# A smaller first piece, and kv spread by SBUF DMAs, in a fused polysketch attention and feed-forward kernel

## The chip, the cores and the metric

The kernel runs on one core of a Trainium2 chip. The metric is device time in microseconds (us) of one execution, as the median of several runs. PE is the matrix engine (PEld its weight loads), DVE the vector engine, ACT the scalar engine, POOL the general engine, SP the engine that issues most DMAs.

## The reference

Attention with a quadratic feature map instead of a softmax, for 4 batches, 4 heads, 1088 tokens and head size 32, followed by a feed-forward block on the joined heads (4352 tokens, 128 columns, inner width 2048). S1 and S2 have 8 rows each.

```python
def phi(x):
    a = np.einsum('rd,bhsd->bhsr', S1, x)
    b = np.einsum('rd,bhsd->bhsr', S2, x)
    return np.einsum('bhsi,bhsj->bhsij', a, b).reshape(*x.shape[:-1], r * r)
q_p, k_p = (phi(q), phi(k))
kv = np.einsum('bhsf,bhsd->bhfd', k_p, v)
z = np.sum(k_p, axis=2)
num = np.einsum('bhsf,bhfd->bhsd', q_p, kv)
den = np.einsum('bhsf,bhf->bhs', q_p, z)[..., None] + 1e-06
x = (num / den)            # heads joined: (4352, 128)
h = x @ w_in
out = (h - np.tanh(h)) @ w_out
```

## The kernel before

The kernel records every operation with its reads and writes, and a table of tokens (TABLE) gives the order: "66t:0" puts operation 66 on the tensor engine and takes choice 0 of the buffer that it opens; v, a, g and s are DVE, ACT, POOL and SP; F and f are filler products of 512 and 256 columns. `plan` hands out the buffers in that order and `sync` sets the waits. Nothing is scheduled at run time: each engine works through its list in order, and SP's list is one queue of DMA issues. CAP limits the bytes of the large loads in flight: a load waits for the one that lies that many bytes back.

*Key side of a batch.* k is transposed in 32x32 blocks on DVE (kT, L536), PE makes the sketches a and b (L581), DVE transposes them back (abk, L593), PE makes the gram matrix for the denominator (L608, L618 or L620), DVE and POOL make the outer products w in three parts (L648), and PE multiplies them with v into a small matrix pv (L663), in which partitions are (head, v column) and columns the 64 features, in two halves of 32.

*kv_tail.* To use pv as the stationary matrix of the numerator, it has to be transposed, and each head's block is wanted on all four quadrants of 32 partitions, since the features of token block g lie on quadrant g. So ACT or DVE copies pv to kvd with each half repeated four times along the columns (128x256), PE transposes the two 128x128 halves (L681), and ACT or DVE copies the result to kvb.

*Query side.* q is transposed (L573), sketched by PE (L759), transposed back into abc (L764), divided by the denominator (L776 to L784), its outer products formed on POOL or DVE (qp, L802), transposed (qpT, L807), and the numerator formed by PE in 32x32 tiles: 32 products per batch, for two halves x of the features, four heads h (column strips of the array) and four token groups g (row strips), in the order x, h, g (L818). Two copies then write x transposed as bf16 into xT.

*Batch 0* is split: its first 12 column blocks (384 tokens) go through `q_heads`, which uses a block-diagonal kv made from pv by a DVE transpose (kvh, L691) and a masked product (kve, L692), and full-array products (L706, L737). The rest (192 columns per token group) takes the path of the other batches. So the feed-forward block can begin on 384 tokens.

*Feed-forward.* Groups of 384, 352, 352, six times 512, and 192 tokens (GCOLS). For each group and each of 16 blocks of the inner width: h (PE, L923) into one of three PSUM banks, tanh (ACT, L927), and, in an order of the table, the product with w_out (L944); the linear part h @ w_out comes from W_in x W_out made once (wc, L901, from transposed weights wiT, L887), as a high and a low bf16 part (L948). In groups 5 to 8 DVE adds h to tanh for some columns instead (L932). The output is transposed by DVE (ot, L953) and stored by four DMAs per group and batch.

*Fillers.* Before the feed-forward work begins PE runs products of zeros into bank 3 (L429, L430), 26 of 512 columns and 8 of 256; their operand zz is cleared by DVE first.

Of the kernel before, what the change touches and what calls it, by code (L numbers as in the profile page):

```python
# [4 lines left out]
B, H, S, D = 4, 4, 1088, 32  # L5
# [7 lines left out]
FP32 = mybir.dt.float32  # L13
# [5 lines left out]
GCOLS = [384, 352, 352] + [512] * 6 + [192]  # L19
CAP = 1.45e6  # L20
PAIRS = 7
GDIR = {5: 192, 6: 320, 7: 320, 8: 320}
CUT0 = [0, 12, 34]
PIECES = {0: [(3, 9)], 1: [(0, 9)], 2: [(0, 9)], 3: [(0, 9)]}
ENGINES = {"v": "vector", "a": "scalar", "g": "gpsimd", "t": "tensor", "s": "sync"}
TABLE = """
0v 15a 16s 18s 17s 56g 1g 10g 2g 14g 9g 13g 3g 6v 4v 5v 50v:0 12g 65g 58g 51v 54v 53v 52v 55g 7g 59g 19s 23s 22a 30s
21s F F F F F F F F F F F F 66t:0 84v 67t 69v:0 68t 70v F F F F f 71t:0 29s 20s 57g 8g 25s 72a:0 F f 73t 74a 24a 61g
27s 34s 64v 77v:0 76v:1 26s F F 85t:1 35s 78g:2 28s 107v 31s 75v 86v:0 87g:0 230a 88v:0 89v:0 90v:0 f 79t:0 80t 111t:0
81t 82v 33s F F F F F 238t:0 91v:0 92v:0 83g 229a 112v:1 42s 43s 32s 108a:0 95g:1 113g:0 96v:1 232g 40s 38s F f 237t  # L30
36s 39s 41s 114v:0 115v:0 f 109t f 93t:1 44s 37s 116g:0 239a 117g:0 119g:1 234g 231a f 97t:2 94v 110a:0 236g f 240t:0
124v:0 98a 45s 105s 100s 125v F 249t:1 250a:0 241t 253t:2 254a:1 251t:1 252a:2 233a 126t:0 255t:2 242v 48s 46s 257t:1
273t:0 128v:0 256a:3 281t:0 282t 283t 127v 279t:2 63g 129t:0 274a:4 259t:0 120v:0 258a:0 284t 261t:1 130v:0 118v 285t
280a:1 131t 243t:2 244t 99s 103s 101s 47s 102s 49s 104s 260a:2 262a:3 277t:0 263t:1 132v:0 121t:0 60g 133v 159v:0
278a:0 269t:0 160v 286t 136g:0 106s 264a:5 271t:1 235a 134v:1 123v 245t 122a 246t 270a:6 247a 161t:0 248v 135v:2
267t:0 265t:2 162v:1 272a:2 324t:1 266a:7 325a:8 62g 268a:9 137t:2 138t 139t 163v 169g:3 308t:1 170g:0 143v 140a:0
359t:0 309a:10 287t 288t 141t 360a:3 142a:0 316t:1 318t:2 317a:5 289t 275t:0 144t:0 178v 145v:0 146g:0 11g 147v:0
276a:7 319a:11 320t:1 290t 306t:0 291t 381t:2 292t 293t 321a:12 314t:1 307a:9 389t:0 382a:6 315a:2 294t 295t 304t:2
296t 390a:4 312t:1 305a:0 297t 298t 313a:7 299v:0 148v:0 332t:0 149v:0 164t:0 333a:1 165a:0 310t:2 311a:13 371t:1
336t:0 166t 367t:0 337t 328t:2 338t 339t 372a:0 167v:0 168v 322t:1 368a:14 329a:9 323a:10 179t:0 377t:0 330t:1 378a:13  # L40
150v:0 151v:0 326t:2 154g:1 327a:15 331a:16 340t 341t 342t 343t 152g:0 373t:0 374a:2 344t 387t:2 345t 180v:1 388a:5
334t:1 346t 335a:7 181g:0 347t 365t:0 348t 385t:2 366a:8 349t 386a:9 363t:1 350t 351t 352t 353t 369t:0 361t:2 155v
364a:1 153v 375t:1 376a:10 370a:7 362a:11 156t:0 383t:0 354v:1 379t:1 158a 391t:0 392t 182v:0 393t 157v 183v:0 394t
384a:12 430t:2 194v:0 380a:3 395t 418t:0 396t 431a:1 195v 414t:1 397t 444t:2 398t 399t 419a:8 400t 401t 436t:0 415a:0
402t 438t:1 403t 404t 184g:0 187v:0 213v 445a:2 432t:2 405t 406t 407t 408t 302s 437a:7 473t:0 439a:3 185g:1 433a:6
409v:2 428t:1 416t:2 171v:1 196t:0 474a:4 422t:0 446t:0 417a:5 429a:9 420t:2 434t:1 411s 172t:2 412s 197v:0 173t 198v
199t:0 174t 186v:0 189g:2 190v 205g:2 421a:10 424t:2 423a:0 435a:11 175a:0 200v:0 425a:12 447t 471t:0 472a:5 201t
440t:1 188v 176t 448t 426t:2 441a:13 357s 413s 410s 300s 489t:0 449t 450t 202v:0 203v 427a:8 490a:10 177v:0 442t:1
481t:2 214t:0 475t:0 451t 482a:0 443a:14 477t:2 206v:0 476a:15 452t 453t 487t:0 204v:1 478a:12 454t 499t:1 497t:2 455t
488a:8 456t 483t:0 457t 458t 215v:0 216v:0 217v:0 500a:9 218v:0 498a:16 469t:1 495t:2 459t 356s 219g:0 484a:1 485t:0  # L50
224v:0 225v:1 486a:6 470a:7 496a:11 191t:0 491t:0 222g:1 192v 220g:0 460t 493t:1 461t 462t 193a 524t:2 492a:17 463t
530t:0 223v 494a:3 479t:1 525a:13 464v:2 207t:0 465s 301s 531a:2 526v 208t 545t:2 501t:0 532v 536t:0 480a:14 527t:1
546a:18 221v 547v 537a:7 502t 503t 504t 538v 533t:2 505t 528a:5 506t 539t:0 529v 534a:4 507t 542t:1 540a:12 535v 508t
541v 543a:0 548t:2 509t 303s 510t 544v 560t:0 549a:1 511t 512t 554t:1 561a:14 550v 513t 562v 555a:6 551t:2 514t 552a:8
# [12 lines left out]
775t 791t:1 790t 776t 788t:0 792a:4 787t 803t:2 789a:0 802t 777t 778t 794t:1 793t 804a:5 808t:1 809t 799t:0 810t 800t
795a:1 801a:3 805t:2 806t 779v:1 780s 782s 807a:6 783s 811t 812t 813t 814t 815t 816t 781a 817t 818t 819t 820t 821t
822t 823t 824t 825t 826v:0 827s 829a 828s 830a
# [64 lines left out]
class _Prog:  # L134
# [40 lines left out]
    def plan(self, table, filler):  # L175
# [8 lines left out]
        for token in table.split():  # L184
            at += 1
            if token in "fF":
                o = _Op()
                o.engs, o.fn, o.mode, o.name, o.dma = {"tensor": 0}, filler[0][token], "128x128", "fill", 0
                o.deps, o.users, o.vals, o.lock, o.big = {filler[1]: True}, [], [], False, False
# [140 lines left out]
def bass_polysketch_attn__then__act_tanh_shrink_kernel(  # L330
# [27 lines left out]
    def copy(e, name, o, i):  # L358
# [32 lines left out]
    kvd_p = pool("kvd", 2, [128, 256])  # L391
# [4 lines left out]
    kvb_p = pool("kvb", 4, [128, 2, 128])  # L396
# [29 lines left out]
    zz = sbv("zz", [128, 384], BF16)  # L426

    zop = P.add({"vector": (1.0, 1.0)}, lambda e, n: e.memset(zz.ap[:, :], 0.0), w=[zz], name="zz")  # L428
    filler = ({"f": lambda e, n: e.matmul(bank(3)[:, 0:256], zz.ap[:, 0:128], zz.ap[:, 128:384], start=True, stop=True),  # L429
               "F": lambda e, n: e.matmul(bank(3), zz.ap[:, 0:128], zz.ap[:, None, 128:384].to_broadcast([128, 2, 256]),  # L430
                                          start=True, stop=True)}, zop)
    pb[3].ops.append(zop)
# [96 lines left out]
    kvbv = [_Val(kvb_p) for _ in range(B)]  # L529
# [142 lines left out]
    def kv_tail(b):  # L672
        kvd, kvb = _Val(kvd_p), kvbv[b]
        P.add({**_a(256), **_vp(256)}, lambda e, n: copy(
            e, n, kvd.ap.rearrange("p (x g f) -> p x g f", x=2, g=4),
            pv[b].ap[:, 0:64].rearrange("p (x f) -> p x f", x=2)[:, :, None, :].to_broadcast([128, 2, 4, 32])),
            r=[pv[b]], w=[kvd], name=f"kvd{b}")

        def kvt(e, n):
            for x in range(2):  # L680
                i = e.transpose(pv[b].ap[:, x * 128:(x + 1) * 128], kvd.ap[:, x * 128:(x + 1) * 128], ident.ap[:, :])  # L681
            return i
        P.add(_pe(260, 185.0), kvt, r=[kvd, ident], w=[pv[b]], mode="128x128", name=f"kvt{b}")
        P.add({**_a(256), **_vp(256)}, lambda e, n: copy(
            e, n, kvb.ap.rearrange("p x c -> p (x c)"), pv[b].ap[:, 0:256]),
            r=[pv[b]], w=[kvb], name=f"kvb{b}")

    kvh = _Val(ap=sb("kvh", [128, 64]))

    def kv_heads():  # L690
        P.add(_vp(64), lambda e, n: e.transpose(kvh.ap, pv[0].ap[:, 0:64]), r=[pv[0]], w=[kvh], name="kvh")  # L691
# [154 lines left out]
    def attention():  # L846
# [15 lines left out]
        for b0, b1 in PIECES[0]:  # L862
            q_piece(0, 3, b0, b1, *st)
# [178 lines left out]
```

## Time and profile before

| | |
|---|---|
| median of 3 runs | 104.08 us (103.92 to 104.67) |
| the profiled execution | 103.72 us, span 101.8 us |
| PE busy | 97.0 us (95% of the span) |
| DVE busy | 82.3 us (81%) |
| ACT busy | 80.1 us (79%) |
| POOL busy | 29.8 us (29%) |
| DMA | 11.37 MB, mean 112 GB/s |
| granted PE clock | 1.0 |

The span runs from the first to the last instruction. Lines such as L923 are lines of the kernel; a group of instructions is named by its line, its engine and operation, and the tiles out<-in. A product's length holds the time through the array, so lengths of neighbours overlap; the distance between starts is what a product costs in a stream. The chain of waits is followed back from the last instruction, at each step to what released it.

### The profile page before, as it was taken

How to read it: one execution, taken by the hardware profiler on the slowest of the kernel's cores; microseconds unless marked ns; L12 is line 12 of the kernel's file. 1: busy time of each engine (PE TensorE's matmuls, PEld its weight loads, DVE VectorE, ACT ScalarE, POOL GpSimd, SP SyncE). 2: the span in 40 equal slices, each digit the busy share in tenths (PEclk: the TensorE clock that was granted, in tenths of full speed). 3: DMA queues.
4: the chain of work that ended last, by engine and by line, in shares of the span. 5: the costliest groups of instructions: out<-in, count | busy, mean ns of one | idle time of the engine just before them, and what ended most of it. 6: DMA issues, size and time to landing. Idle time of an engine off the chain costs nothing.

```text
span 101.8 us, 3049 instructions
## 1 busy us (share of the span) xinstructions
PE 97.0 (95%) x1266; PEld 48.9 (48%) x1266; DVE 82.3 (81%) x148; ACT 80.1 (79%) x158; POOL 29.8 (29%) x50
## 2 busy tenths in 40 slices
PE   5999999999999999999999999999999999999960
PEld 2334666365744565554634454344453444444650
DVE  3449799699986996989998898688889788999530
ACT  0311257979799896998999799999979999989940
POOL 5130758963383292255501570000000000000000
PEclk9999999999999999999999999999999999999999
DMA  2898859999989300003400003106002640035445
GB/s 56 249 270 274 311 189 294 328 294 296 333 251 325 99 0 6 0 0 53 79 6 0 0 0 60 29 0 95 0 2 36 101 70 0 0 55 79 76 70 81
DMA packets 25917, 11.37 MB, mean 112 GB/s; under 512 B 19120, under 2 KB 23600, under 8 KB 25904
## 3 DMA queue, kind: packets, MB, share of 16 engines
q1 hardware_dynamic: 24528, 10.64, 40.6%
q10 hardware_dynamic: 1376, 0.54, 2.1%
q8 instruction: 10, 0.16, 0.7%
q14 instruction: 3, 0.02, 0.1%
HBM read 8.95 MB, written 2.23 MB: 110 GB/s over the span
## 4 chain that ended last, share of the span: by engine, by line
PE 95%; DVE 1%; ACT 0%; issue 0%
PE psb L923 31%; PE psb L944 29%; PE psb L430 9%; PE psb L818 6%; PE psb L663 5%; PE psb L581 3%; PE psb L948 3%; PE psb L759 3%; PE psb L737 1%; PE psb L608 1%; PE psb L901 1%; PE psb L429 1%; PE psb L681 1%; PE psb L706 1%; PE psb L887 1%; PE psb L618 1%
## 5 line engine op out<-in xcount | busy, mean ns | idle before, releaser
L927 ACT ACTIVATE th<-psb 128x512 bf16<-128x512 f32 (+3 forms) x135 | 70.3, 605 | 5.0 <-PE psb L923 4.3
L923 PE MATMUL psb<-xT,wi 128*128 128x512 bf16 (+3 forms) x160 | 47.3, 349 | 0.2 <-ACT th L927 0.2
L944 PE MATMUL psb<-th,wo 128*128 128x512 bf16 (+3 forms) x159 | 43.4, 347 | 0.0
L932 DVE TENSOR_TENSOR th<-psb,th 128x320 bf16<-128x320 f32 (+2 forms) x47 | 25.8, 558 | 4.5 <-ACT th L927 2.4
L923 PEld LDWEIGHTS psb<-xT,wi 128*128 128x128 bf16 x160 | 14.7, 98 | 22.8 <-ACT th L927 7.8
L944 PEld LDWEIGHTS psb<-th,wo 128*128 128x128 bf16 x159 | 15.3, 98 | 10.2 <-DVE ot L953 0.4
L802 POOL TENSOR_TENSOR qp<-ap,abc 128x768 f32<-128x768 f32 x8 | 12.0, 1511 | 6.9 <-DVE qp L802 5.4
L807 DVE STREAM_TRANSPOSE qpT<-qp 128x768 f32<-128x768 f32 x11 | 10.5, 962 | 0.2
L430 PE MATMUL psb<-zz 128*128 128x512 bf16 x26 | 9.3, 497 | 1.1 <-DVE zz L428 1.1
L648 POOL TENSOR_TENSOR w<-abk 128x768 f32<-128x768 f32 x5 | 7.5, 1517 | 8.4 <-DVE w L648 4.3
L953 DVE STREAM_TRANSPOSE ot<-psb 128x512 f32<-128x512 f32 (+3 forms) x10 | 6.2, 625 | 2.6 <-PE psb L944 2.6
L536 DVE STREAM_TRANSPOSE kT<-kL 128x576 f32<-128x576 f32 (+3 forms) x10 | 5.6, 600 | 1.4 <-DMA kL<-in_k_dram 1.4
L648 DVE TENSOR_TENSOR w<-abk 128x768 f32<-128x768 f32 x7 | 6.5, 947 | 0.1
L818 PE MATMUL psb<-qpT,kvb 32*32 32x288 f32 (+1 forms) x256 | 6.1, 392 | 0.0
L573 DVE STREAM_TRANSPOSE qT<-qL 128x1088 f32<-128x1088 f32 (+2 forms) x5 | 5.2, 1065 | 0.5 <-DMA qL<-in_q_dram 0.5
L663 PE MATMUL psb<-w,vL 128*32 128x64 f32 x288 | 5.4, 221 | 0.0
L764 DVE STREAM_TRANSPOSE abc<-psb 128x1152 f32<-128x1152 f32 (+1 forms) x4 | 5.0, 1262 | 0.4 <-PE psb L759 0.4
L663 PEld LDWEIGHTS psb<-w,vL 128*32 128x32 f32 x288 | 4.4, 110 | 2.0 <-issue 1.7
L430 PEld LDWEIGHTS psb<-zz 128*128 128x128 bf16 x26 | 2.8, 120 | 4.9 <-issue 3.1
L593 DVE STREAM_TRANSPOSE abk<-psb 128x288 f32<-128x288 f32 x8 | 3.4, 462 | 1.5 <-PE psb L581 1.5
L359 ACT ACT_TABLE_LOAD x1 | 1.3, 1283 | 4.2 <-DMA kL<-in_k_dram 4.2
L784 POOL TENSOR_TENSOR ap<-abc,rd 128x288 f32<-128x288 f32 (+1 forms) x3 | 1.9, 630 | 9.2 <-DVE rd L782 9.2
(90 smaller groups left out, 79.0 us busy)
## 6 DMA issues: line engine op xcount, KB each, us to landing
kL<-in_k_dram SPq DMA_DIRECT2D x8, 272.0 KB, 4.4
vL<-in_v_dram SPq DMA_DIRECT2D x15, 144.0 KB, 4.1
qL<-in_q_dram SPq DMA_DIRECT2D x6, 272.0 KB, 4.4
wo_f<-in_moe_w_out_dram SPq DMA_DIRECT2D x4, 256.0 KB, 4.1
out_dram<-ot SPq DMA_DIRECT2D x15, 64.0 KB, 2.0
wi_f<-in_moe_w_in_dram SPq DMA_DIRECT2D x3, 256.0 KB, 4.0
out_dram<-ot SPq DMA_DIRECT2D x8, 48.0 KB, 2.5
qL<-in_q_dram SPq DMA_DIRECT2D x2, 176.0 KB, 3.9
```

The source lines that it names most:

```text
L430: "F": lambda e, n: e.matmul(bank(3), zz.ap[:, 0:128], zz.ap[:, None, 128:384].to_broadcast([128, 2, 256]), start=True, stop=True)}, zop)
L536: P.add(_v(nb * 32 * (r1 - r0)), lambda e, n, e_=e_, nb=nb, r0=r0, r1=r1: e.transpose(kTv[b][r0].ap.rearrange("p (j u t r) -> p r j u t", ...
L648: P.add({**_v(768), **_gt(768)}, lambda e, n: e.tensor_tensor(out=wv.ap.rearrange("p (x i j) -> p x i j", i=8, j=8), in0=abh(0)[:, :, :, N ...
L663: i = e.matmul(pv[b].ap[h * 32:(h + 1) * 32, 0:64], vL[b][:, h, blk * 32:(blk + 1) * 32], wvs[b, p].ap[:, (bi * 4 + h) * 64:(bi * 4 + h + ...
L802: P.add({**_v(cn * 256), **_gt(cn * 256)}, lambda e, n, qp=qp, c0=c0, cn=cn: e.tensor_tensor(out=qp.ap[:, 0:cn * 256].rearrange("p (x i j) ...
L807: P.add(_v(cn * 256), lambda e, n, qp=qp, o0=o0, cn=cn: e.transpose(qt.ap[:, o0 * 256:(o0 + cn) * 256], qp.ap[:, 0:cn * 256]), r=[qp], w=[ ...
L818: i = e.matmul(psa4[h * 32:(h + 1) * 32, g, 0:nb * 32], kvb.ap[g * 32:(g + 1) * 32, x, h * 32:(h + 1) * 32], qq[g * 32:(g + 1) * 32, 0:nb, ...
L923: P.add(_mm(n_), lambda e, n, jb=jb, hv=hv: e.matmul(hv.ap[:, jb % m * 512:jb % m * 512 + n_], wi[jb // 4].ap[:, (jb % 4) * 128:(jb % 4 + ...
L927: act = P.add(_a(n_ * m), lambda e, n, hv=hv, th=th: e.activation(out=th.ap.rearrange("p (u x) -> p u x", u=m)[:, :, 0:n_], in_=hv.ap.rear ...
L932: P.add(_vp(gc * m), lambda e, n, hv=hv, th=th: e.tensor_tensor(out=th.ap.rearrange("p (u x) -> p u x", u=m)[:, :, 0:gc], in0=hv.ap.rearra ...
L944: fn = lambda e, n, x=x, st=st, sp_=sp_: e.matmul(ov.ap[:, 0:n_], wo[x // 4].ap[:, x % 4, :], ths[x][0].ap[:, ths[x][1] * 512:ths[x][1] * ...
L953: P.add(_vp(n_), lambda e, n: e.transpose(ot.ap[:, 0:n_], ov.ap[:, 0:n_]), r=[ov], w=[ot], name=f"ot{gi}")
```

## The change

1. `GCOLS` is 256, 416, 416 for the first three groups instead of 384, 352, 352. Batch 0's first piece is 8 column blocks (256 tokens) instead of 12, the rest 7 blocks (224 columns per token group) instead of 6.
2. `kv_tail` no longer repeats, transposes on PE and copies. DVE transposes pv in 32x32 blocks into slot 0 of a [128, 4, 64] tile (for batch 0 this is the kvh that existed already). Then six SBUF-to-SBUF DMAs per batch (128 - 32r and 32r partitions, 256 bytes per partition, for r = 1, 2, 3) fill slots 1 to 3 with the same rows shifted by r quadrants. The numerator takes head h for group g from slot (g - h) mod 4.
3. The numerator's 16 tiles are walked in another order in batches 0 (along diagonals), 2 (g outside, h inside) and 3 (reversed in the second half); batch 1 keeps h outside, g inside.
4. The fillers read a constant zero of one column, repeated, instead of zz, and wait for nothing. zz shrinks to 32 columns. 11 instead of 12 fillers stand ahead of the first k sketch.
5. CAP is 2.0 MB instead of 1.45 MB.
6. TABLE is new. The mask product wqd goes from DVE to POOL; one of batch 0's three w goes to DVE between the denominator and its reciprocal; the spread DMAs are on SP's queue, for batch 0 between the loads of k for batch 1 and those of w_out and k for batch 2; all four loads of w_in are on ACT's queue; the loads of the rest of q stand ahead of those of v. Both copies of wiT are on ACT, the casts of w_out are split over POOL, DVE and ACT, and all w of batches 1 to 3 are on POOL.

```diff
-GCOLS = [384, 352, 352] + [512] * 6 + [192]
-CAP = 1.45e6
+GCOLS = [256, 416, 416] + [512] * 6 + [192]
+CAP = 2.0e6
...
-CUT0 = [0, 12, 34]
-PIECES = {0: [(3, 9)], 1: [(0, 9)], 2: [(0, 9)], 3: [(0, 9)]}
+CUT0 = [0, 8, 34]
+PIECES = {0: [(2, 9)], 1: [(0, 9)], 2: [(0, 9)], 3: [(0, 9)]}
...
-    zz = sbv("zz", [128, 384], BF16)
+    zz = sbv("zz", [128, 32], BF16)
...
+    zc = nc.const_aps.tensor(0.0, [128, 1], FP32).bitcast(BF16)[:, 0:1]
+    fill = lambda n_: lambda e, n: e.matmul(bank(3)[:, 0:n_], zc.to_broadcast([128, 128]), zc.to_broadcast([128, n_]), start=True, stop=True)
+    filler = {"f": fill(256), "F": fill(512)}
...
-    kvbv = [_Val(kvb_p) for _ in range(B)]
+    kvbv = [_Val(ap=sb("kvb", [128, H, 64])) for _ in range(B)]
+    kvhv = [_Val(ap=x.ap[:, 0, :]) for x in kvbv]
...
     def kv_tail(b):
-        kvd, kvb = _Val(kvd_p), kvbv[b]
-        P.add({**_a(256), **_vp(256)}, lambda e, n: copy(
-            e, n, kvd.ap.rearrange("p (x g f) -> p x g f", x=2, g=4),
-            pv[b].ap[:, 0:64].rearrange("p (x f) -> p x f", x=2)[:, :, None, :].to_broadcast([128, 2, 4, 32])),
-            r=[pv[b]], w=[kvd], name=f"kvd{b}")
...
-        P.add(_pe(260, 185.0), kvt, r=[kvd, ident], w=[pv[b]], mode="128x128", name=f"kvt{b}")
-        P.add({**_a(256), **_vp(256)}, lambda e, n: copy(
-            e, n, kvb.ap.rearrange("p x c -> p (x c)"), pv[b].ap[:, 0:256]),
-            r=[pv[b]], w=[kvb], name=f"kvb{b}")
+        kvh, kvb = kvhv[b], kvbv[b]
+        if b:
+            P.add(_vp(64), lambda e, n: e.transpose(kvb.ap[:, 0, :], pv[b].ap[:, 0:64]), r=[pv[b]], w=[kvh], name=f"kvh{b}")
+        for r in range(1, H):
+            for j, (d0, s0, n_) in enumerate(((r * 32, 0, 128 - r * 32), (0, 128 - r * 32, r * 32))):
+                P.add({"sync": 480.0, "scalar": 400.0}, lambda e, n, r=r, d0=d0, s0=s0, n_=n_: e.dma_start(
+                    out=kvb.ap[d0:d0 + n_, r, :], in_=kvb.ap[s0:s0 + n_, 0, :]), r=[kvh], w=[kvb], dma=(n_ * 256, n_), name=f"kvs{b}.{r}{j}")
...
             for x in range(2):
-                for h in range(4):
-                    for g in range(4):
-                        i = e.matmul(psa4[h * 32:(h + 1) * 32, g, 0:nb * 32],
-                                     kvb.ap[g * 32:(g + 1) * 32, x, h * 32:(h + 1) * 32],
-                                     qq[g * 32:(g + 1) * 32, 0:nb, h, x, :], start=(x == 0), stop=(x == 1))
+                for i in range(16):
+                    u, w = i // 4, i % 4
+                    h, g = ((w, (u + w) % 4), (u, w), (w, u), (u if x == 0 else 3 - u, w if x == 0 else 3 - w))[b]
+                    r = e.matmul(psa4[h * 32:(h + 1) * 32, g, 0:nb * 32],
+                                 kvb.ap[g * 32:(g + 1) * 32, (g - h) % 4, x * 32:(x + 1) * 32],
+                                 qq[g * 32:(g + 1) * 32, 0:nb, h, x, :], start=(x == 0), stop=(x == 1))
...
-        st = q_front(0, 3, 9)
+        st = q_front(0, 2, 9)
```

115 lines of the change are left out of this document (52 added, 63 removed).

## The prediction

> **What bounds the kernel now.** I read the page first (busy shares), then busy time by stage, then the chain that ended last in order of time.
>
> ```profile
> PE 97.0 (95%) x1266; PEld 48.9 (48%) x1266; DVE 82.3 (81%) x148; ACT 80.1 (79%) x158; POOL 29.8 (29%) x50
> ```
> ```profile
> 85.00:95.00 10.00, 10.00 (x53) 4.74 (x51) 9.47 (x13) 9.68 (x11) 0.00 (x0) 1.00 0.25 39
> ```
> ```profile
> 16.80 0.22 PE psb L887 x4
> 17.24 0.21 PE psb L923
> 17.48 0.50 ACT th L927
> 18.02 0.34 PE psb L923
> 18.36 0.76 PE psb L581 x16
> ...
> 20.36 0.30 PE psb L608 x18
> ...
> 21.42 0.29 PE psb L618 x2
> 21.71 0.45 PE psb L901 x8
> ...
> 22.48 1.22 PE psb L818 x59
> ...
> 25.50 0.58 PE psb L923 x3
> ...
> 27.95 0.22 PE psb L681 x2
> ...
> 88.47 0.86 PE psb L944 x4
> ```
>
> The page says PE is busy for 95%. The stage row (columns: window, sum, then PE, PEld, DVE, ACT, POOL) shows it full late in the run, with ACT and DVE just behind. The last chain row gives the pace: 0.86 us for four products of 512 columns, 0.215 each, 0.42 ns per column. So the span has three parts: a lead until the first feed-forward product can start (17.1 us, the 17.24 row being its later part), a body in which PE works almost without holes, and a tail of copy and stores from 98.4 that the change leaves alone. Holes in the body appear only near its start: between 17.48 and 18.02 PE waits for the first tanh. Later pieces follow each other within about 0.1 us.
>
> How large is the hole in the first stage? Until the first product of group 1 (inside the 25.50 piece, at about 25.75) PE does 21 products of 384 columns (21 x 0.162 = 3.4), the fourth weight transpose 0.22, two k sketches 1.52, gram 0.30 and 0.29, W_in x W_out 0.90, batch 0's numerator 1.22: 7.85 us in 8.65. Its holes are 0.8 us.
>
> **The lead.** Columns: start, length, instruction.
>
> ```profile
> 1.12 5.30 PE L430 MATMUL psb<-zz 128*128 128x512 bf16 x12 [1.12 <-DVE zz L428]
> 5.23 0.24 POOL L545 TENSOR_TENSOR wab<-stt,mask 128x32 f32<-128x32 f32 x1
> 6.35 1.10 PE L581 MATMUL psb<-kT,wab 64*32 64x144 f32 x32
> 7.51 0.85 DVE L593 STREAM_TRANSPOSE abk<-psb 128x288 f32<-128x288 f32 x2 [0.79 <-PE psb L581]
> 8.39 1.83 DVE L648 TENSOR_TENSOR w<-abk 128x768 f32<-128x768 f32 x2
> 10.13 0.91 DVE L573 STREAM_TRANSPOSE qT<-qL 128x704 f32<-128x704 f32 x1
> 10.30 1.52 POOL L648 TENSOR_TENSOR w<-abk 128x768 f32<-128x768 f32 x1 [4.30 <-DVE w L648]
> 11.05 0.57 DVE L709 STREAM_TRANSPOSE abc<-psb 128x384 f32<-128x384 f32 x1
> 14.14 0.94 DVE L764 STREAM_TRANSPOSE abc<-psb 128x768 f32<-128x768 f32 x1
> 15.14 0.58 DVE L730 STREAM_TRANSPOSE qpTh<-qp 128x384 f32<-128x384 f32 x1
> 15.77 0.92 PE L737 MATMUL psb<-qpTh,kvd 128*128 128x192 f32 x4
> 16.73 0.32 ACT L359 CAST xT<-psb 128x192 bf16<-128x192 f32 x1 [0.21 <-PE psb L737]
> ```
>
> *Fillers.* They no longer wait for the memset, and 11 instead of 12 stand ahead of the first k sketch. At 5.30/12 = 0.44 each, from 0.84 (when DVE's memset shows the engines released), they end near 5.7. The sketch's weights are ready at 5.47 (row wab), so it starts near 5.7 instead of 6.35: 0.65 earlier. The fillers run at 0.44 where a warm product takes 0.215: the clock is low until about 6.4. If it rises at the same instant as before, the sketch's first 0.7 us runs at half pace, 0.35 lost; if the rise moves along, nothing. I take half: 0.5 earlier. The Trainium skill, "TensorE: Matmul & The Clock Gate", Part 1, says that the clock rises after a busy window of about 3.4 us whose phase is free-running. By that rule the rise may stay where it was, and the gain at this step would be 0.3 instead of 0.65; the trace agrees that 5 us of fillers can stay slow.
>
> *Batch 0's first 256 tokens.* abk ends at 7.9 (8.36 before). On DVE then stand one w (0.92) instead of two, with the mask product gone to POOL; qT of 832 columns (0.91 x 832/704 = 1.08); sc 0.17; abc starts near 10.05 instead of 11.05 and takes 0.41. m on POOL waits for its w (1.52 from 8.9) and ends at 10.8; den 0.25, the moved w 0.92, rd 0.2, abc of batch 0's rest now ahead (896 columns, 1.1), kv transpose 0.24: 13.5. Then qph, m, qpTh, den, qpTh at 0.3 to 0.42 each (256-wide, against 0.58): 15.4. The last numerator (128 columns, 0.6), a DVE copy 0.23: first product near 16.5 against 17.1, **-0.60**. Bounds: -0.9 (clock and PE both early) and 0 (the moved w and abc eat the gain). Loads: all four wi now leave on ACT's queue, two of them before its table load, and q's rest ahead of v. v's last piece leaves at about 5.9 instead of 6.6, but shares the engines with the two wi; I cost this at nothing, the cover being w on POOL until 10.4; without it each us late counts fully.
>
> **The kv spread.**
>
> ```profile
> L359 ACT COPY kvd<-psb x3: 366/372/373, 14.1 to 49.1; 128x256 f32<-128x256 f32 x3
> L359 ACT COPY kvb<-psb x3: 377/378/391, 16.1 to 74.1; 128x256 f32<-128x256 f32 x3
> 13.60 1.49 SPq L465 DMA_DIRECT2D wo_f<-in_moe_w_out_dram  x3
> 17.35 1.75 SPq L465 DMA_DIRECT2D vL<-in_v_dram  x2
> out_dram<-ot SPq DMA_DIRECT2D x4, 8.0 KB, 2.3
> kL<-in_k_dram SPq DMA_DIRECT2D x8, 272.0 KB, 4.4
> ```
>
> It removes two PE transposes per batch (0.22, the L681 row above); batches 1 to 3 lie in the full body: **-0.66**. It removes 3 x 0.37 + 3 x 0.38 = 2.3 us from ACT and 0.8 from DVE, and adds three kv transposes (0.24 each) to DVE: not on the path, since PE leads. Batch 0's numerator takes 224 columns instead of 192, +0.11 (32 columns x 4 passes x 2 rounds at 0.42 ns). It adds 24 DMAs. SP waits for kv, issues three, a wo load, one, a wo load, and two more: eight issues of 0.5 (1.49/3) from 13.6 end at 17.6; with landing between 2.3 (8 KB row) and 4.4 (large loads ahead of it) the spread is there at 20 to 22. The numerator is due at 21.5 (below), so the cover is thin. Behind SP's wait stand lwo0, about 1 us later than its 13.6, then wo, k and v of batches 1 and 2; their users come 2 us and more after landing, so zero; if that cover is gone, o0.0 waits for wo0. For batch 1 the spread is interleaved with 12 loads from 28 on, done by 37, against a numerator at about 39; batches 2 and 3 have an idle queue.
>
> **The smaller group 0.**
>
> ```profile
> L927 ACT ACTIVATE th<-psb 128x512 bf16<-128x512 f32 x63 | 33.2, 602 | 2.0 <-PE psb L923 1.7
> L927 ACT ACTIVATE th<-psb 128x352 bf16<-128x352 f32 x32 | 12.5, 473 | 1.0 <-PE psb L923 0.9
> 19.42 2.42 ACT L927 ACTIVATE th<-psb 128x384 bf16<-128x384 f32 x6
> L359 ACT COPY wiT<-psb 128x1024 bf16<-128x1024 bf16 x1 | 1.0, 1012 | 0.2 <-PE psb L887 0.2
> 17.18 2.98 POOL L802 TENSOR_TENSOR qp<-ap,abc 128x768 f32<-128x768 f32 x2
> ```
>
> The columns add up to the same, so the total of products and tanh is unchanged. But a 256-wide product costs PE 0.108 while its tanh costs ACT about 0.30 start to start (0.39 for 384, (2.42-0.49)/5, less 128 columns at (602-473)/160 = 0.8 ns). The order of the built kernel shows what ACT does from first tanh to the numerator's copy: 14 tanh (4.2), the second wiT copy (1.0, moved from DVE), gm 0.2, a wo cast 0.6, the copy 0.5: 6.5, plus some 0.6 waiting for products. The numerator itself waits for qp on POOL (three from 15.7 to 19.4), its transposes, a wo cast moved to DVE (0.5) and scx: 21.5. Group 1 then starts at 24.05, 7.55 us after the first product. PE's work there: 16 x 0.108 + 6 x 0.108 + 0.22 + 0.76 + 0.30 + 0.29 + 0.45 + 1.33 = 5.7. Holes 1.8 against 0.8 before: **+1.0**, since the second k sketch and half of W_in x W_out now come later. From 24 on PE has work queued at every step and ACT has 2 us less than before; I add nothing.
>
> **Order inside the numerator.**
>
> ```profile
> 28.81 0.77 PE L759 MATMUL psb<-qT,wq 32*32 32x288 f32 x32
> 56.54 1.60 PE L818 MATMUL psb<-qpT,kvb 32*32 32x288 f32 x64
> ```
>
> Batches 0, 2 and 3 walk the 16 tiles in other orders. Bounds per batch: -0.2 (two rounds at the q sketch's 0.70 to its next start, for 1.53), +0.24 (half a pass of drain between the rounds). I take 0, nearest to the unchanged batch 1.
>
> **Sum.** -0.60 - 0.66 + 0.11 + 1.0 = -0.15 us. The profiled execution took 103.72 (span 101.8 and 1.9 around it), 0.36 under the median of 104.08; so 103.57 for such an execution, and 103.9 for the median.
>
> **Rivals** (against the median; 1%, 1.04 us, is about what this measurement tells from no change.)
> - *No starving*: tanh and POOL keep pace, the holes stay at 0.8, and the lead gains 0.75 (half way to its bound): -0.75 - 0.66 + 0.11 = -1.3, **102.8**. For it: ACT loses 2.3 us of copies. Against: its order there is full.
> - *The spread lands late* (the other side): SP issues can take 0.87 (1.75/2) instead of 0.5. Then the last leaves at 20.6, lands at 23 to 25, and PE, which takes work in order, stands behind the numerator for 1.5 to 3.5 us: **105.5** at the low end. It is slower by 1% once the landing passes 22.9. Against: those slow issues came with waits for older loads.
> - *Short tanh don't pay*: spacing stays at 0.39, 14 x 0.09 more: **105.1**.
> - *The lead is unmoved* (the change doesn't do what it says there): **104.5**.
> - *Two products of one row strip in turn can't overlap*: batch 2's new order keeps four tiles of a strip together, so 48 of 64 half products would each wait 0.24: +11, **115**. The q sketch's 0.77 for 32 in just that order speaks against it. The Trainium skill, "TensorE: Matmul & The Clock Gate", Part 3, states such a rule for weight loads; the q sketch's row contradicts it.
>
> **How the numbers follow.** Forecast 0.44 (own range 103.3 to 104.7), no starving 0.27, spread late 0.13, lead unmoved 0.08, short tanh 0.07, strips 0.01. The range 102.3 to 105.3 leaves out the later spread, the strips and the best of the first rival, under 0.2. Faster by over 1% (below 103.04): the first rival and the forecast's edge, 0.30. Slower (above 105.12): late spread, strips, half of short tanh and the edges, 0.20. Within: 0.50.
>
> **What would show it.** First k sketch near 5.7; first product at 16.5; in the stage after it, PE holes near 1.8 us and 256-wide tanh 0.30 apart; first product of 416 columns near 24; the numerator of batch 0 released by scx, not by a DMA; no L681; numerators at 1.53. A numerator that waits for a DMA, or a body with holes after 25 us, would make the prediction wrong.

## The result, and the profile after

The changed kernel is slower: 108.44 us (median of 4 runs, 107.77 to 108.96) beside 104.38 us for the kernel before on the same chip, a ratio of 1.0415 with a 95% interval of 1.0355 to 1.0474. The forecast of 103.9 and its range up to 105.3 both missed. The profiled execution took 108.21 us with a span of 105.9, against 103.72 and 101.8 before: 4.1 us more span. The first feed-forward product (the expert product of the expectations below) starts at 17.34 instead of 17.10 (+0.2), PE's last product ends at 102.0 instead of 98.4 (+3.4 in the body), and the tail of stores takes 0.5 more.

Busy shares of the changed kernel, and below them the chain that ended last, by engine and by line:

```profile
PE 95.1 (90%) x1246; PEld 48.1 (45%) x1256; DVE 78.7 (74%) x147; ACT 79.3 (75%) x153; POOL 34.5 (33%) x53
...
PE 26%; SPq 19%; DVE 18%; DMA 14%; ACT 9%; POOL 6%; issue 4%; DVEq 0%
SPq L462 12%; PE psb L936 10%; ACT th L919 9%; PE psb L915 8%; DMA vL<-in_v_dram 6%; PE psb L810 4%; DMA qL<-in_q_dram 4%; POOL w L646 4%; DVE qpT L798 4%; DVE abc L755 3%; DMA out_dram<-ot 3%; SPq L955 3%; SPq L677 3%; DVE ot L945 3%; DVE th L924 2%
```

PE was busy for 97.0 us and is now for 95.1: the work did fall, and yet the run is longer, so the difference is idle time. The chain says where to look: SP's queue (SPq; line 462 issues the loads) and DMAs hold 33% of the path.

The same stages of both kernels (window, sum, then PE, PEld, DVE, ACT, POOL; the last three numbers are granted clock, DMA share and GB/s), before first:

```profile
10.00:15.00 5.00, 5.00 (x128) 3.11 (x128) 4.33 (x11) 1.80 (x4) 3.17 (x4) 1.00 0.73 259
15.00:20.00 5.00, 4.80 (x46) 2.79 (x45) 4.18 (x10) 4.29 (x10) 4.58 (x6) 1.00 0.99 295
20.00:25.00 5.00, 5.00 (x122) 3.11 (x126) 4.74 (x10) 4.32 (x12) 3.02 (x7) 1.00 0.94 297
25.00:30.00 5.00, 5.00 (x137) 2.71 (x122) 4.64 (x8) 4.26 (x13) 2.90 (x2) 1.00 0.96 303
```
```profile
10.00:15.00 5.00, 3.67 (x119) 2.42 (x119) 3.44 (x9) 2.10 (x4) 1.76 (x7) 1.00 0.69 224
15.00:20.00 5.00, 4.62 (x49) 2.64 (x45) 4.63 (x12) 3.52 (x8) 4.04 (x5) 1.00 0.33 87
20.00:25.00 5.00, 4.79 (x107) 3.08 (x108) 2.63 (x7) 4.22 (x15) 1.71 (x4) 1.00 0.79 233
25.00:30.00 5.00, 3.82 (x81) 2.24 (x82) 2.60 (x6) 3.09 (x9) 4.09 (x3) 1.00 1.01 344
```

Before, the loads ran at 295 to 303 GB/s from 15 to 30 us. After, 87 GB/s flow between 15 and 20 us: about 1 MB, or 3.5 us of that stream, is not loaded there (208 GB/s times 5 us). PE pays between 25 and 30 us, with 3.82 us busy out of 5. SP's own queue in the changed kernel shows why (start, length, instruction):

```profile
14.23 1.81 SPq L677 DMA_DIRECT2D kvb<-kvb  x3
16.08 0.58 SPq L462 DMA_DIRECT2D wo_f<-in_moe_w_out_dram  x1
16.71 0.54 SPq L677 DMA_DIRECT2D kvb<-kvb  x1
17.29 1.51 SPq L462 DMA_DIRECT2D wo_f<-in_moe_w_out_dram  x1
18.85 1.17 SPq L677 DMA_DIRECT2D kvb<-kvb  x2
20.06 1.14 SPq L462 DMA_DIRECT2D wo_f<-in_moe_w_out_dram  x2
21.24 0.98 SPq L462 DMA_DIRECT2D kL<-in_k_dram  x2
```

SP issued a load of k at 9.93, then stood at the spread's first DMA until kv was there at 14.2, and then took 0.53 to 0.60 us for each spread DMA, with the loads in between and behind. The first load of wo left at 16.08 (13.60 before), batch 2's k at 21.24. In the kernel before that was 15.13:

```profile
15.13 0.98 SPq L465 DMA_DIRECT2D kL<-in_k_dram  x2
```

Of these 6.1 us some 1.0 are one slow issue (1.51 at 17.29, where a load of wo takes 0.5 to 0.6 elsewhere), and 0.5 is a load of wo that the new order puts ahead of k. Those who waited, each with its idle time and releaser in brackets:

```profile
26.59 1.37 DVE L534 STREAM_TRANSPOSE kT<-kL 128x576 f32<-128x576 f32 x2 [2.05 <-DMA kL<-in_k_dram]
28.01 0.83 PE L579 MATMUL psb<-kT,wab 64*32 64x288 f32 x16 [1.18 <-DVE kT L534]
```
```profile
11.63 0.54 PE L661 MATMUL psb<-w,vL 128*32 128x64 f32 x24 [1.17 <-DMA vL<-in_v_dram]
```
```profile
60.34 0.88 PE L810 MATMUL psb<-qpT,kvb 32*32 32x288 f32 x33 [0.96 <-DVE qp L793]
```

Batch 2's k sketch stands 1.18 us for k, batch 0's kv product 1.17 us for v, and batch 2's numerator 0.96 us. For the last the profile names a VectorE product that ended at 60.25. The numerator doesn't read that one (it belongs to batch 3, and the transpose that it does read was done at 57.4); it waits for the six spread DMAs of batch 2, the last of which landed at 60.25 too, 0.09 us before the start.

### The profile page after: what moved, and what is told of

It reads as the page before. It is cut to its first block, busy times and chain, and to the rows that moved or that the text cites. A ratio compares the mean times of both kernels' runs of the same rounds, so it can differ in the third digit from the quotient of the medians.

```text
span 105.9 us, 3059 instructions
## 1 busy us (share of the span) xinstructions
PE 95.1 (90%) x1246; PEld 48.1 (45%) x1256; DVE 78.7 (74%) x147; ACT 79.3 (75%) x153; POOL 34.5 (33%) x53
## 4 chain that ended last, share of the span: by engine, by line
PE 26%; SPq 19%; DVE 18%; DMA 14%; ACT 9%; POOL 6%; issue 4%; DVEq 0%
SPq L462 12%; PE psb L936 10%; ACT th L919 9%; PE psb L915 8%; DMA vL<-in_v_dram 6%; PE psb L810 4%; DMA qL<-in_q_dram 4%; POOL w L646 4%; DVE qpT L798 4%; DVE abc L755 3%; DMA out_dram<-ot 3%; SPq L955 3%; SPq L677 3%; DVE ot L945 3%; DVE th L924 2%
## 5 line engine op out<-in xcount | busy, mean ns | idle before, releaser
L919 ACT ACTIVATE th<-psb 128x512 bf16<-128x512 f32 (+4 forms) x135 | 70.4, 606 | 6.9 <-PE psb L915 5.8
L646 POOL TENSOR_TENSOR w<-abk 128x768 f32<-128x768 f32 x10 | 14.9, 1512 | 6.9 <-DVE scx L626 4.1
L793 POOL TENSOR_TENSOR qp<-ap,abc 128x768 f32<-128x768 f32 (+1 forms) x8 | 11.0, 1402 | 10.0 <-DVE qp L793 9.0
L798 DVE STREAM_TRANSPOSE qpT<-qp 128x768 f32<-128x768 f32 (+1 forms) x12 | 10.8, 913 | 0.1
L428 PE MATMUL psb<-const-float32-0.0 128*128 128x512 bf16 (+1 forms) x30 | 9.8, 443 | 1.1 <-PEq L1019 0.8
L534 DVE STREAM_TRANSPOSE kT<-kL 128x512 f32<-128x512 f32 (+3 forms) x10 | 5.7, 603 | 4.1 <-DMA kL<-in_k_dram 4.1
L359 ACT CAST wi<-wi_f 128x512 bf16<-128x512 f32 x4 | 2.5, 618 | 4.0 <-DMA wi_f<-in_moe_w_in_dram 3.8
L359 DVE CAST xT<-psb 128x128 bf16<-128x128 f32 (+3 forms) x6 | 3.2, 536 | 2.8 <-issue 1.8
L428 PEld LDWEIGHTS psb<-const-float32-0.0 128*128 128x128 bf16 x32 | 3.1, 112 | 4.4 <-issue 3.7
L810 PEld LDWEIGHTS psb<-qpT,kvb 32*32 32x32 f32 x256 | 3.4, 103 | 3.0 <-DVE qp L793 1.2
```

The source lines that it names most:

```text
L428: fill = lambda n_: lambda e, n: e.matmul(bank(3)[:, 0:n_], zc.to_broadcast([128, 128]), zc.to_broadcast([128, n_]), start=True, stop=True)
L646: P.add({**_v(768), **_gt(768)}, lambda e, n: e.tensor_tensor(out=wv.ap.rearrange("p (x i j) -> p x i j", i=8, j=8), in0=abh(0)[:, :, :, N ...
L793: P.add({**_v(cn * 256), **_gt(cn * 256)}, lambda e, n, qp=qp, c0=c0, cn=cn: e.tensor_tensor(out=qp.ap[:, 0:cn * 256].rearrange("p (x i j) ...
L798: P.add(_v(cn * 256), lambda e, n, qp=qp, o0=o0, cn=cn: e.transpose(qt.ap[:, o0 * 256:(o0 + cn) * 256], qp.ap[:, 0:cn * 256]), r=[qp], w=[ ...
L810: r = e.matmul(psa4[h * 32:(h + 1) * 32, g, 0:nb * 32], kvb.ap[g * 32:(g + 1) * 32, (g - h) % 4, x * 32:(x + 1) * 32], qq[g * 32:(g + 1) * ...
L919: act = P.add(_a(n_ * m), lambda e, n, hv=hv, th=th: e.activation(out=th.ap.rearrange("p (u x) -> p u x", u=m)[:, :, 0:n_], in_=hv.ap.rear ...
```

## The experiments

Two theories were held against each other. Theory 1: the spread's DMAs on SP (a wait, then 0.6 us an issue) delay the loads, and land late themselves. Theory 2: the first group of 256 columns gives PE too little to do. Names: lwo, lwi, lk, lq, lv are the loads of w_out, w_in, k, q, v (batch.piece); kvs0.20 is one of batch 0's six spread DMAs. All ratios are to the kernel before, run on the same chip.

### The changed kernel with one thing moved

**Loads ahead of batch 0's spread.**

```diff
 SP queue
-kvs0.20 kvs0.21 kvs0.11 lwo0 kvs0.31 lwo1 kvs0.30 kvs0.10 lwo3 lwo2 lk2.0 lk2.1
+lwo0 lwo1 lwo3 lwo2 lk2.0 lk2.1 kvs0.20 kvs0.21 kvs0.11 kvs0.31 kvs0.30 kvs0.10
```

> The changed kernel with one edit: batch 0's six spread DMAs stand on SP behind the four loads of wo and the two of batch 2's k, instead of ahead of and between them. Theory 1 (SP's one queue: its wait for batch 0's kv, 10.3 to 14.2 us, and the 0.6 us that each of the spread's six issues takes delay every load behind them) expects the first of the wo loads to be issued near 12 to 14 us instead of 16.1, batch 2's k to land by 21.5 instead of 25.9 and 26.6, the 1.24 us of idle TensorE ahead of batch 2's k sketch to be gone, and with it 1.2 to 1.7 us of the time: 106.7 to 107.2. Theory 2 (the smaller first group starves TensorE, whatever the loads do) expects 108.1 to 108.5. If batch 0's spread now lands after 22 us, num0.2 waits for it and up to 1 us of the gain is lost; both would show in the trace.

Measured: 106.56 us, ratio 1.0229 (1.0176 to 1.0282), beside 1.0415 for the changed kernel. SP's queue and the first wait behind it:

```profile
10.96 2.06 SPq L462 DMA_DIRECT2D wo_f<-in_moe_w_out_dram  x4
13.82 1.44 SPq L462 DMA_DIRECT2D kL<-in_k_dram  x2
15.30 4.63 SPq L677 DMA_DIRECT2D kvb<-kvb  x6
```
```profile
28.20 1.31 DVE L571 STREAM_TRANSPOSE qT<-qL 128x1088 f32<-128x1088 f32 x1 [0.65 <-DMA qL<-in_q_dram]
```

The order of twelve DMAs is worth 1.9% of the time; of the single moves it is the only one whose interval is well clear of the changed kernel's. Batch 2's k sketch no longer waits (25.76 instead of 28.01). But the six issues took 4.63 us here (one of them 1.50; in the changed kernel the six add up to 3.5), and now stand ahead of q and v: the wait moved on to q. In the profiled execution v landed sooner as well (10.94 instead of 11.54, with the queue up to there as in the changed kernel), and the first feed-forward product came at 16.74 instead of 17.34; so up to 0.6 us of the gain in that one execution is not the order's.

**v ahead of w_in.**

```diff
-lwi1, lwi0 on ACT's queue at 4.35 and 5.00 us
+lwi1, lwi0 on SP's queue behind lv0.2
```

> The changed kernel with one edit: the two loads of w_in that ScalarE issued at 4.35 and 5.00 us are issued by SP behind the last piece of batch 0's v. Theory 1 (the order of the loads decides: v's last pieces landed at 11.0 and 11.5 because 0.5 MB of w_in went beside them) expects v to land by 10.3, the kv product to start at 10.5 instead of 11.6, the first expert product 0.8 to 1.0 us sooner and 107.4 to 107.7 in all. A rival (the bytes decide, not the order: q's rest lands late in any case, or w_in is now what the lead waits for) expects v no earlier than 11.2 and 108.2 to 108.6.

Measured: 107.61 us, ratio 1.0334 (1.0262 to 1.0405). v's last piece landed at 9.28 instead of 11.54, the kv product started at 9.97 instead of 11.63 and the first feed-forward product at 15.77 instead of 17.34. As theory 1 had it for the lead, but of 1.57 us there only about 0.8 is left at the end: batch 2's k sketch waited 1.04 us again. And the 17.34 is one draw: in the profile of the next experiment, whose lead is that of the changed kernel, v landed at 10.46 and the first feed-forward product came at 16.27. Against that one the order is worth 0.5 us in the lead.

**Spreads of batches 1 and 2 in a row.**

```diff
 SP queue
-kvs1.21 lv2.0 kvs1.31 kvs1.10 lk3.1 lk3.0 lv3.1 lq3.0.0 lq3.0.1 kvs1.11 kvs1.30 kvs1.20
+kvs1 (all six) lv2.0 lk3.1 lk3.0 lv3.1 lq3.0.0 lq3.0.1
-st0.0 st2.2 st1.3 kvs2.11 st0.3 kvs2.21 kvs2.30 kvs2.31 kvs2.20 kvs2.10
+kvs2 (all six) st0.0 st2.2 st1.3 st0.3
 VectorE
-scx3 qpT2.6 kvh2
+scx3 kvh2 qpT2.6
```

> The changed kernel with batch 1's six spread DMAs issued in a row (five loads of batch 3 behind them instead of between them), batch 2's transpose of kv on VectorE ahead of a 1 us transpose instead of behind it, and batch 2's six in a row ahead of one store. Theory 1 (the numerators of batches 1 and 2 wait for the spread's last landing: 41.74 against a start at 41.83, 60.25 against 60.34) expects batch 1 landed by 37.5 with its numerator no longer released by a DMA, batch 2 landed by 58.5 to 59, the 0.96 us hole ahead of batch 2's numerator gone or below 0.3, and 107.4 to 107.8 in all. Theory 2 (the holes are starved work that only moves) expects holes of the same size elsewhere and 108.1 to 108.5.

Measured: 107.38 us, ratio 1.0288 (1.0203 to 1.0373). Batch 1's spread landed at 37.78 instead of 41.74, far ahead of its numerator, and no hole is left ahead of batch 2's numerator, though it still starts just after the landing (59.97 after 59.87). The interval overlaps the changed kernel's, so the 1.0 us is likely but not certain. Batch 2's six stand ahead of four stores here, not of one as the expectation says.

**The spread undone.** kv of all batches goes through copy, two PE transposes and copy again, as in the kernel before; the rest stays as changed.

```diff
-kvh1..3 (VectorE transpose), kvs0..3 (24 DMAs)
+kvd0..3 (copy), kvt0..3 (two PE transposes each), kvb0..3 (copy)
```

> The changed kernel with the spread undone for all four batches: kv goes through copy, two TensorE transposes and copy again as in the kernel before; pieces, groups, fillers and the order of everything else stay as changed (only two PSUM banks are picked otherwise). It adds 0.22 us of TensorE work for batches 1 to 3 and some for batch 0. Theory 1 (the spread's place in SP's queue is the loss: it holds the loads up, 87 GB/s between 15 and 20 us against 295 in the kernel before, and its late landings hold two numerators) expects the loads to run on, minus 1.9 and minus 1.0 as the two reorderings gave, plus 0.7: 105.7 to 106.6; what stays above the kernel before is v's late landing and the smaller first group. Theory 2 (the smaller first group alone) expects 108.5 to 109.3.

Measured: 107.21 us, ratio 1.0336 (1.0294 to 1.0377): the loads run on (267 GB/s between 15 and 20 us), yet only a fifth of the loss comes back, and the time lies between the two theories' numbers. Part of what is missing may come from where the copies stand: ACT takes its work in order, and the copy ahead of batch 1's transposes held later tanh up until the kv product was there.

```profile
29.02 0.37 ACT L359 COPY kvd<-psb 128x256 f32<-128x256 f32 x1 [1.01 <-PE psb L663]
```
```profile
29.87 0.35 PE L922 MATMUL psb<-xT,wi 128*128 128x416 bf16 x1 [0.91 <-ACT th L926]
```

**The three moves together.**

> The changed kernel with the three reorderings of the earlier experiments together: batch 0's spread behind the loads of wo and of batch 2's k, w_in behind v, and the spreads of batches 1 and 2 in a row. Theory 1 (all of the loss but the smaller group's starvation is the order of DMAs) expects the gains to add: minus 1.4, minus 0.9, minus 0.8, so 105.0 to 105.8, and what stays above the kernel before (some 1 us) is the starvation of the smaller first group, 2.0 us of holes between 17 and 25 us against 0.8. Theory 2 expects 107.5 or more.

Measured: 106.00 us, ratio 1.0194 (1.0141 to 1.0247). The time lies above the 105.0 to 105.8 that was expected, and together the moves are not better than the first one by more than the intervals allow. In the profiled execution the first feed-forward product started only at 17.89, after 1.99 us of an idle PE:

```profile
17.89 0.40 PE L915 MATMUL psb<-xT,wi 128*128 128x256 bf16 x2 [1.99 <-DVE kT L534]
```

Its weights had been loaded at 15.84, and x, the one thing that the program lets it wait for, was done at 15.8. So neither v nor w_in held it, and no wait in the profile ends near 17.89; the cause is open. (ACT's cast of the third piece of w_in waited 2.17 us for its load, but it did so in the changed kernel too.) The granted clock was 0.81 in the stage from 15 to 20 us and 0.85 in the next. From the first feed-forward product to the last product of PE this execution took 81.9 us, against 84.7 in the changed kernel and 81.3 in the kernel before: most of what the body had lost is back, though a late start also gives the loads time. What the 1.9% that stay over the kernel before are made of, this run doesn't tell.

### The kernel before with one part of the change

**Fillers alone.** Fillers read a constant, 11 instead of 12 ahead of the k sketch.

```diff
-"F": e.matmul(bank(3), zz.ap[:, 0:128], ...)      # waits for the memset of zz
+"F": e.matmul(bank(3), zc.to_broadcast([128, 128]), zc.to_broadcast([128, 512]), ...)
```

> The kernel before with one part of the change alone: the TensorE fillers read a constant instead of a zeroed tile, so they wait for nothing, and one of the twelve ahead of the k sketch is left out. If the lead follows its start (k sketch at 5.7 instead of 6.35, v landed at 9.96 in the kernel before, so its kv product can move), the time falls by 0.3 to 0.65: 103.7 to 104.1. A rival (the k sketch is held by its input's transposes, or the kv product by v at 9.96 and w) expects 104.2 to 104.5.

Measured: 103.97 us beside 104.26, ratio 1.0007 (0.9964 to 1.0051): nothing. In its trace the first feed-forward product starts at 16.26 instead of 17.10, and the gain is gone twelve microseconds later:

```profile
27.24 2.50 DVE L572 STREAM_TRANSPOSE qT<-qL 128x1088 f32<-128x1088 f32 x2 [1.24 <-DMA qL<-in_q_dram]
```
```profile
28.70 0.93 PE L758 MATMUL psb<-qT,wq 32*32 32x288 f32 x32 [0.81 <-DVE qT L572]
```

Batch 1's q sketch starts at 28.70 against 28.81 before. The load of q sets it, not the lead.

**Spread alone, for batches 1 to 3.** The DMAs stand behind the last load, after the first eight stores, and ahead of the stores near 69 us.

> The kernel before with the kv spread alone and for batches 1 to 3 alone, its eighteen DMAs put where SP has nothing else to issue: behind the last load (near 31.4 us), between the first eight stores and the rest (near 50 us), and ahead of the stores near 69 us. Batch 0 keeps its TensorE transposes. Theory 1 (the spread itself is worth the 0.66 us of TensorE that it removes, and only its place in the queue made it a loss) expects landings at 37, 57 and 74.5 us ahead of the numerators at 39, 56.5 and 75, and 103.6 to 104.0, some 0.4 to 0.7 below the kernel before. Theory 2 (the spread costs in itself: longer issue, slow landing) expects the numerators to wait for their DMAs again and 104.4 to 106.

Measured: 105.75 us, ratio 1.0128 (1.0084 to 1.0172), slower. The places were bad in two ways:

```profile
39.64 0.76 PE L827 MATMUL psb<-qpT,kvb 32*32 32x288 f32 x29 [0.93 <-DMA kvb<-kvb]
```
```profile
77.48 0.72 DVE L963 STREAM_TRANSPOSE ot<-psb 128x512 f32<-128x512 f32 x1 [1.93 <-DMA out_dram<-ot]
```

Batch 1's six landed at 39.55, after three load issues ahead of them had taken 1.2 to 1.4 us each, and batch 3's six pushed two stores back whose output buffer VectorE needed at 75.5.

**The same, placed better.**

```diff
 SP queue
-lv2.3 lv3.1 lv3.3 kvs1 (six) ... st0.0 st1.1 kvs2 (six) ... kvs3 (six) st1.3 st4.0 st3.2 st4.3 st1.0
+kvs1 (six) lv2.3 lv3.1 lv3.3 ... kvs2 (six) st0.0 st1.1 ... st1.3 st1.0 kvs3 (six) st4.0 st3.2 st4.3
```

> The kernel before with the spread for batches 1 to 3, as in the earlier run that lost 1.3%, but batch 1's six ahead of the last three loads, batch 2's ahead of two stores, batch 3's behind two stores whose late landing had held an output buffer up (1.93 us of VectorE). Theory 1 (place only) expects no numerator to be released by a DMA, the 0.93 and 1.40 us holes gone, and minus 0.3 to minus 0.66: 103.6 to 104.1. The rival (the DMAs cost something wherever they stand) expects new holes of the same size and 104.6 to 105.8.

Measured: 104.69 us beside 104.07, ratio 1.0035 (0.9992 to 1.0077). Both holes are gone and PE's last product ends at 98.0 (98.4 before), yet no gain can be measured. The spread's cost was its place; its worth, 0.66 us of PE, has not shown up in the time.

**Fillers and spread; fillers and q; all.** The first is the fillers with the badly placed spread; the second moves lq1.0.1 ahead of lq2.0.0; the third has the well placed spread as well.

> The kernel before with both: fillers from the constant, one fewer ahead of the k sketch, and the spread for batches 1 to 3 in the same places. If the two gains are apart from each other, 103.1 to 103.7; if the spread's landings hold the numerators once these come 0.5 us sooner, 103.7 to 104.2.

> The kernel before with the fillers from the constant, and the second half of batch 1's q loaded ahead of the first half of batch 2's q. With the fillers alone the first product came 0.84 us sooner and nothing was left of it at batch 1's q sketch, which waited 0.81 us for its q (VectorE's transpose 1.24 us for the DMA). If it is this one load, its move keeps 0.4 to 0.8 us: 103.4 to 103.9. If the stream of loads as a whole is the bound up to 31 us (295 GB/s without a gap), the next load is late instead: 104.0 to 104.4.

> The two together: fillers from the constant, batch 1's q sooner, the spread well placed. If the gains add: 102.8 to 103.6. If the rivals of the two parts hold: 104.4 or more.

Measured: 1.0119 (1.0064 to 1.0174), 1.0024 (0.9981 to 1.0066) and 0.9981 (0.9940 to 1.0022; 103.92 us beside 104.07). Nothing adds up to a gain. In the first's profiled execution the first feed-forward product came at 18.19, PE having waited 1.81 us for ACT's cast of w_in, which had waited 3.58 us for its load: the lead too hangs on a load.

**Groups alone.**

```diff
-GCOLS = [384, 352, 352] + [512] * 6 + [192]
+GCOLS = [256, 416, 416] + [512] * 6 + [192]
```

> The kernel before with the column groups 256, 416 and 416 in place of 384, 352 and 352, and nothing else (piece 0 stays 384 tokens, the order stays). Theory 2 (a first group of 256 columns gives TensorE 1.9 us less to do before batch 0's numerator, and the work waits behind it) expects the first 416-column product to start no more than 0.9 us sooner instead of 1.9, more holes between 17 and 26 us, and 105.0 to 106.1. Theory 1 alone (only the queue counts) expects 103.9 to 104.6.

Measured: 105.73 us, ratio 1.0124 (1.0073 to 1.0174): +1.3 us, theory 2's number. From its first feed-forward product (16.47) to its first one of 416 columns (24.94) it takes 8.5 us, against 8.7 before, though group 0's 21 products there are 1.1 us shorter (128 columns less, at 0.42 ns). Then it meets the same load:

```profile
27.62 2.51 DVE L573 STREAM_TRANSPOSE qT<-qL 128x1088 f32<-128x1088 f32 x2 [1.24 <-DMA qL<-in_q_dram]
```
```profile
29.08 0.87 PE L759 MATMUL psb<-qT,wq 32*32 32x288 f32 x32 [0.86 <-DVE qT L573]
```

Batch 1's q sketch starts between 28.7 and 29.1 in this kernel, in the one before and in the one with other fillers, though their first feed-forward products lie 0.8 us apart. Work that is moved from group 0, which PE can do until then, into groups 1 and 2 is done after it: from there to the first product of 512 columns it takes 14.5 us instead of 12.8 (29.08 to 43.55, 28.81 to 41.58).

**The held queue alone.** The kernel before, with batch 0's kv spread where the change puts it; batches 1 to 3 keep their PE transposes.

```diff
 SP queue
-lk1.1 lwo0 lwo1 lwo3 lk2.0 lk2.1 lwo2
+lk1.1 kvs0.20 kvs0.21 kvs0.11 lwo0 kvs0.31 lwo1 kvs0.30 kvs0.10 lwo3 lk2.0 lk2.1 lwo2
```

> The kernel before with batch 0's kv alone spread by DMAs, which stand on SP where the change puts them: ahead of the loads of wo and between them, so SP waits for kv (near 13.2 us) and issues six more DMAs of 0.6 us before batch 2's k. Batches 1 to 3 keep their TensorE transposes. Theory 1 (each microsecond that the stream of loads stands still before 31 us comes back as TensorE waiting for batch 1's q or batch 2's k) expects the loads 1.5 to 3.5 us later, VectorE waiting 1 to 3 us for q, and 105.0 to 106.5, though TensorE has 0.4 us less to do. The rival (loads have slack) expects 103.9 to 104.5.

Measured: 106.93 us, ratio 1.0253 (1.0213 to 1.0292): +2.6 us, with one pair of PE transposes (0.22 us) less to do; the expectation's 0.4 was too much. Its stage rows (columns as above) and the wait:

```profile
15.00:20.00 5.00, 4.80 (x48) 2.96 (x46) 3.80 (x9) 4.17 (x9) 4.65 (x6) 1.00 0.63 176
```
```profile
29.57 2.50 DVE L574 STREAM_TRANSPOSE qT<-qL 128x1088 f32<-128x1088 f32 x2 [1.93 <-DMA qL<-in_q_dram]
31.03 0.99 PE L765 MATMUL psb<-qT,wq 32*32 32x288 f32 x32 [1.11 <-DVE qT L574]
```

The stream falls from 295 to 176 GB/s, batch 2's k is issued at 18.19 instead of 15.13, the last load of all lands at 38.1 instead of 35.1, and the q sketch starts at 31.03 instead of 28.81 (31.20 in the changed kernel). The spread itself is no wait here: it landed at 20.71, and batch 0's numerator starts at 23.07. The time is 0.4 us above theory 1's range.

**More loads in flight.** The third of the kernels above, with CAP at 2.0e6 as in the change.

> The kernel before with fillers from the constant, batch 1's q sooner, the spread for batches 1 to 3 well placed, and loads in flight up to 2.0 MB instead of 1.45 MB, as the change has it. If the loads' pauses between 10 and 15 us (259 GB/s against 295 later) hold the body, this fills them: 102.8 to 103.6. If not, 103.8 to 104.2 as without it.

Measured: 104.96 us, ratio 1.0037 (1.0005 to 1.0069). No gain, rather a loss of a few tenths. None of the versions tried beats the kernel before by more than its interval.

## Why the prediction was wrong

**The step that failed** is the sentence "Behind SP's wait stand lwo0, about 1 us later than its 13.6, then wo, k and v of batches 1 and 2; their users come 2 us and more after landing, so zero". The prediction added up eight issues but then costed only the first load behind them. The eight issues ended at 20.0 instead of 17.6, and the delay grows down the queue: 2.5 us at the first load of wo, 6.1 us at batch 2's k. And the cover of 2 us is each load's own slack, while the loads from 15 to 30 us are one stream at 295 to 303 GB/s, so what one load loses the later ones lose too (3.0 us still at the last load of the held queue alone). Put into the kernel before by itself, this step costs 2.6 us (2.2 to 3.0). In the changed kernel, taking it out gives less back: 1.9% by reordering, 0.8% by undoing the spread; why less, is open. Batch 2's k sketch with its 1.18 us is a body with a hole after 25 us, which the prediction had named as the sign of being wrong. The prediction had a rival for the spread landing late at batch 0's numerator, and a sentence that o0.0 might wait; neither was where it hit in the changed kernel's profile. Batch 0's spread landed by 21.63, and its numerator at 22.38 waited for no DMA. But with the spreads of batches 1 and 2 in a row, where the queue is the same up to there, o0.0 did wait, for the cast of a piece of w_out whose load landed at 20.30:

```profile
21.11 0.27 PE L936 MATMUL psb<-th,wo 128*128 128x256 bf16 x1 [0.88 <-POOL wo L359]
```

**The other spreads**, "batches 2 and 3 have an idle queue" and batch 1 "done by 37", failed too. Batch 1's landed at 41.74, batch 2's at 60.25, because its transpose on VectorE stood behind a transpose of 1 us and one of the six issues took 1.68. Batch 3's was in time.

**The lead** (-0.60 predicted, +0.24 found in the one profile) went wrong at "I cost this at nothing, the cover being w on POOL until 10.4". v shared the DMA engines with w_in and landed at 11.54, and the kv product stood 1.17 us for it. How late v is changes from one execution to the next, though. With the same loads in the lead it landed at 10.46 and 10.94 (the spreads in a row, the loads first); the kv product stood 0.27 and 0.96 us, and the first feed-forward product came at 16.27 and 16.74, about the 16.5 foretold. In the kernel before the lead varies too: not 17.10 but 16.47, 16.88 and 16.95 in three kernels with the same loads and fillers there (the groups alone, the spread alone twice). So the +0.24 is one draw. What repeats is that v is late: 0.3 to 1.2 us of an idle PE, where the prediction had nothing. With v ahead of w_in the first feed-forward product came at 15.77. The Trainium skill, "DMA: Bandwidth & Descriptors", section "Issuing engines are not separate DMA queues", says that DMAs from different engines interleave on the same 16 DMA engines; v's 9.28 without w_in beside it and 10.46 to 11.54 with it agree.

**The fillers** (sketch near 5.7; 5.55 found) were right in place and wrong in worth. Four kernels with the old fillers began the k sketch between 5.63 and 5.94 (the spread alone, badly and well placed, the groups, the held queue), where the profile of before had 6.35. In one of them the fillers ran at 0.43 us to the seventh and at 0.216 from the ninth on, in the kernel before at 0.43 to the end: there the clock happened to rise late. The Trainium skill, "TensorE: Matmul & The Clock Gate", Part 1, has a window of free-running phase; these starts agree. The row that the prediction read as the lead's length was one draw of it.

**The smaller group** (+1.0) was right: between the first product and the first one of 416 columns the holes came to 2.0 us (17.34 to 25.08, for 5.7 us of work by the prediction's count) against the 1.8 foretold, and alone it costs 1.3 us (0.8 to 1.8). The reason was only half seen. The prediction had tanh and the numerator's chain; the trace of the groups alone adds that the next stage begins at a time set by a load, so the work postponed into it is not caught up.

**The kv transposes** (-0.66): PE's busy time did fall, but placed well in the kernel before they gave nothing measurable, -0.1 to +0.8%. **The order inside the numerators** (0) held: in the run with the loads first, batches 1, 2 and 3 in their three orders take 1.52, 1.52 and 1.54 us to the next start, against 1.53, 1.54 and 1.53 in the kernel before.

Sum: the held queue 2.6 and the group 1.3 make 3.9 us, the size of the whole loss of 4.1. They overlap with the late v and the late spreads of batches 1 and 2, for which 0.8 and 1.0 us came back when moved, so the four are not to be added. How the 4.1 divides among all of them to the tenth stays open, as does why the three moves together gave back no more than 2.2%. The rest of the new order, such as all w of batches 1 to 3 on POOL (34.5 us busy instead of 29.8), was not tried by itself.

## What to carry to other kernels

Before a DMA that must wait for a result is put on a queue that also feeds the loads, list every load behind it with the time at which it was issued before: the hold is paid by those behind it when the loads run as one stream without pauses. A stage that starts when a load lands doesn't move when what precedes it gets faster, so work saved ahead of it was worth nothing here (0.84 us in the lead of the fillers alone), and work moved from ahead of it to behind it cost 1.3 us. A single profile's lead is one draw: leads with the same loads differed here by up to 1.1 us, so compare several before a gain is read from one. Read the GB/s of each stage as well as the waits: a stage at a third of the rate, here 87 against 295 GB/s, names the cause ten microseconds before PE stalls.

## What the runs showed of the hardware

From issue to landing a spread DMA took 1.7 us at best and 4.2 at worst in the changed kernel, and its issue took SP 0.52 to 1.68 us (median 0.59), for 8 to 24 KB. The slowest landing was right behind loads of batch 3, but one of 3.7 us had only stores and spread DMAs ahead of it. The Trainium skill, "DMA: Bandwidth & Descriptors", in the section named above, calls the time to initiate a DMA "usually small relative to the DMA itself"; here six of them in a row took SP 4.63 us, and the last had landed 1.3 us after SP was through with it (21.19). Single issues of 1.0 us and more occur in every trace, in the kernel before too (1.10, 1.41 and 2.01 us), with no wait shown.
